# Attention and MLP on one core: x's loads spread over six head pairs, a head pair's loads moved behind the bias phase, and four small reorderings

## The chip, the cores and the metric

One core of a Trainium2 chip runs the whole program. The metric is the device time of one execution in microseconds (us); lower is better. Two times of this kernel that lie within 0.2% of each other can't be told apart.

## The reference, cut to what matters

Attention with a bias that a small network makes from relative positions, then an MLP with ELU over the attention's output (2304 tokens of 512). Sizes: batch 4, 8 heads, 576 positions, head size 64, hidden 32 for the bias, 2048 for the MLP.

```python
scores = (q @ k.transpose(0, 1, 3, 2)) / np.sqrt(D)
psi_rel = np.log1p(np.abs(pos[:, None] - pos[None, :]))
psi_i = np.log1p(np.maximum(pos[:, None], 1.0))
x = (psi_rel / psi_i)[..., None]
bias = np.maximum(x @ w1 + b1, 0.0) @ w2             # [576, 576, heads]
attn = softmax(scores + bias)                        # with the row maximum subtracted
x = (attn @ v) as [2304, 512]
h = x @ w_in
out = np.where(h > 0.0, h, np.exp(np.minimum(h, 0.0)) - 1.0) @ w_out
```

## The kernel before

The program is written in one order by hand (`manual_schedule`): each engine runs its instructions in the order of the code, and an instruction that waits holds all behind it on its engine. SP issues nearly all transfers, so SP is one queue in that sense too.

**Bias phase** (`bias_phase`). 36 sets. `relu(s)` makes four `rel` tiles of a set, one on ACT and three on DVE; `mix(s)` multiplies them on PE; `place(s)` scales the result on ACT with a column of `inv` into a `bo` tile (four buffers of two sets). Every second set a store of 576 KB moves `bo` to `bias` in SBUF; the sets 16 to 19 go to `biast` in smaller stores. Ahead of the loop stand the loads of the first head pairs' `kk` and `qq` (`load_pair`, five transfers of 576 KB in all for a pair) and of `vv` (`load_v`), the first two sets' `relu`, and four DVE copies that spread `inr` into `inv`. Behind the loop stands the load of the first block of MLP weights (`raw`, 1 MB).

**Attention** (`attention`). 16 head pairs `n`, each in five steps `i`. A step computes scores on PE (`ps`), adds the bias and takes the row minimum of the negated sum on DVE (`ss`, `nm`, line 303), takes exp on ACT, transposes on PE (`trans_p`) with copies back by ACT and DVE, and multiplies with v for the pair before (`pv`, `wv`, `xs`), whose result goes to HBM (`xd`). `sm` holds row sums; `turn` writes their reciprocals of a batch to `rd` every fourth pair. In between `decode` unpacks one weight block per pair: DVE reads `raw` (`low`, line 259; `sign`, line 263) and SP may load the next `raw` only after that.

**x for the MLP.** The first 768 tokens of x are four quarters `(r, h)`. `load_x(0, r, h)` loads a quarter of `xd` and the reciprocals `rr` of its rows (one `rr` buffer for all): three transfers for `h = 0`, nine for `h = 1`. `scale_x` multiplies them on DVE. `high_x` and `low_x` split a quarter in two parts. The table `early` says after which step these stand: the key `(-4, 1)` means the fourth pair from the end, pair 12, after step 1.

**MLP** (`mlp`). PE multiplies through `eight` (two blocks) and `seven` (the rest). `elu_next` runs two ACT operations on a product, `elu` the DVE operation of line 751, which is also the last reader of the product's bank. `aside(k)` runs planned side work after each product, among it the steps of `make_w`, which prepares the next weights (`S` sums, `wA`, `wB`). At the end of each third of the tokens six sums `acc` are copied to `os` tiles (even `t` on DVE, odd on ACT) and stored.

Of the kernel before, what the change touches and what calls it, by code (L numbers as in the profile page):

```python
# [10 lines left out]
F32 = mybir.dt.float32  # L11
# [13 lines left out]
def kernel(  # L25
# [11 lines left out]
    nc = tc.nc  # L37
    B, HP, D, _, S = qT.shape
    NT, DM = out.shape
    H = 2 * HP  # L40
    P = 128
# [37 lines left out]
    def w_bank(name):  # L79
        return wp.tile([P, 512], F32, tag="w", name=name)  # L80
# [8 lines left out]
    NP = len(pairs)  # L89
# [3 lines left out]
    def load_pair(n):  # L93
        b, hp = pairs[n]
        kk = ld.tile([P, S], F32, tag="kk", name="kk", bufs=2)
        qq = ld.tile([P, S], F32, tag="qq", name="qq", bufs=2)
        nat[n] = kk, qq

        nc.sync.dma_start(out=kk[0:D], in_=kT[b, hp, :, 0])
        yield  # L100
        nc.sync.dma_start(out=kk[D:P, 0:NCH * P], in_=kT[b, hp, :, 1, TAIL:])
        nc.sync.dma_start(out=kk[D:P, NCH * P:], in_=kT[b, hp, :, 1, 0:TAIL])
        yield
        for e in range(2):
            nc.sync.dma_start(out=qq[e * D:(e + 1) * D], in_=qT[b, hp, :, e])
            yield

    def load_v(n):
        b, hp = pairs[n]
        vv = st["v", n] = ld.tile([P, NU, D], F32, tag="vv", name="vv", bufs=3)  # L110
        nc.sync.dma_start(out=vv, in_=vt[b, hp])


    def bias_phase():
        with (
# [32 lines left out]
            for i in range(4):  # L148
                nc.scalar.dma_start(
                    out=inr[8 * i:8 * i + 8],  # L150
                    in_=cst[32 * i:32 * i + 32, NG + 2 + 4 * H:].rearrange("(s h) n -> h s n", s=4),
                )

            for n in range(2):
                for _ in load_pair(n):
                    pass
            load_v(0)
            w1c, b1c = cs[:, 0:1], cs[:, 1:2]
            W2 = cs[:, 2:]

# [13 lines left out]
            def relu(s):  # L174
                B, x = sets[s]
                rels[s] = []
                for g in range(4):
                    u = RIM - 64 * B - 16 * g - x
                    src = T[:, u:u + S]
                    b = SC[:, 4 * B + g, x:x + 1]  # L180
                    rel = bw.tile([P, S], F32, tag="rel", name="rel")
                    if g == 0:
                        nc.scalar.activation(rel, src, AF.Relu, bias=b)  # L183
                    else:
                        nc.vector.tensor_scalar(rel, src, b, 0.0, op0=ALU.add, op1=ALU.max)
                    rels[s].append(rel)
# [34 lines left out]
                        nc.sync.dma_start(out=biast[q0:q0 + 61:4], in_=src[:, o])  # L221

            AHEAD = 2
            for s in range(AHEAD):
                relu(s)
            for g in range(4):
                q = slice(32 * g, 32 * g + 32)
                nc.vector.tensor_copy(
                    inv[q].rearrange("p b s -> p s b"), inr[0:32].rearrange("p s (b g) -> p s b g", g=4)[:, :, :, g],
                )  # L230
            nc.vector.tensor_scalar(T[:, :cut], T[:, :cut], w1c, None, op0=ALU.mult)
            for s in range(NS):
                mix(s)
# [2 lines left out]
                if s + AHEAD < NS:  # L236
                    relu(s + AHEAD)
            place(NS - 1)
            decode(dp, 0, "load")

# [100 lines left out]
    def trans_p(n, u):  # L343
        pta, ptb = st["pt", n]

        ss = st["ss", n, u]
        if u < NCH:
            dst, o = (pta, u * P) if u < 2 else (ptb, (u - 2) * P)
            banks = [w_bank("wt") for r in range(2)]
            for x in range(2 * NCH):  # L350
                e, j = divmod(x, NCH)
                c = e * (S + TAIL) + j * P
                for r in range(2):
                    q = slice(r * TAIL, (r + 1) * TAIL)
                    nc.tensor.transpose(banks[r][:, x * TAIL:(x + 1) * TAIL], ss[q, c:c + P], ident[q, q])  # L355
            for r in range(2):
                d = dst[:, 0:2 * NCH, o + r * TAIL:o + (r + 1) * TAIL]
                copy = nc.vector.tensor_copy if r == 1 and u % 2 == 0 else nc.scalar.copy
                copy(d, banks[r].rearrange("p (x t) -> p x t", t=TAIL))
                yield  # L360
        else:
            o = 2 * P
            M = NCH * TAIL
            banks = [w_bank("wt") for e in range(2)]
            for j in range(NCH + 1):
                for e, w in enumerate(banks):
                    r = slice(e * TAIL, (e + 1) * TAIL)
                    if j < NCH:
                        c = j * P
                        nc.tensor.transpose(w[:, j * TAIL:(j + 1) * TAIL], ss[r, c:c + P], ident[r, r])  # L370
                    elif e == 0:
                        nc.tensor.transpose(w[r, M:M + TAIL], ss[r, NCH * P:], ident[r, r])
                    else:
                        nc.tensor.transpose(w[:, M:M + TAIL], ss[r, S - P:], ident[r, r])
            for e, w in enumerate(banks):
                r = slice(e * TAIL, (e + 1) * TAIL)
                d = pta[:, e * NCH:(e + 1) * NCH, o:o + TAIL]
                nc.scalar.copy(d, w[:, 0:M].rearrange("p (j t) -> p j t", j=NCH))
                nc.scalar.copy(pta[r, 2 * NCH, o:o + TAIL], w[r, M:M + TAIL])
                yield  # L380
# [123 lines left out]
    xo = dict(zip(("B11", "B12", "B21", "B22"), slots))  # L504
# [5 lines left out]
    def attention():  # L510
# [17 lines left out]

        V, G = nc.vector, nc.gpsimd
        early = {  # L530
            (-5, 3): [(load_x, 0, 0, 0)],
            (-4, 1): [(scale_x, 0, 0, 0, V)],
            (-4, 2): [(load_x, 0, 0, 1)],
            (-4, 4): [(scale_x, 0, 0, 1, V)],
            (-3, 0): [(load_x, 0, 1, 0)],
            (-3, 1): [(high_x, 0, "B11", xo["B11"], V.tensor_copy)],
            (-3, 2): [(scale_x, 0, 1, 0, V)],
            (-3, 3): [(load_x, 0, 1, 1), (low_x, 0, "B11", xo["B11"], V)],
            (-2, 0): [(scale_x, 0, 1, 1, V)],
            (-2, 1): [(high_x, 0, "B12", xo["B12"], V.tensor_copy)],  # L540
            (-2, 2): [(low_x, 0, "B12", xo["B12"], V)],
            (-2, 3): [(high_x, 0, "B21", xo["B21"], V.tensor_copy), (sums_x, 0, ("T1",), G)],
# [87 lines left out]
    def mlp():  # L630
        ep = ctx.enter_context(tc.tile_pool(name="ep", bufs=3))
# [17 lines left out]
        FIRST = 2  # L649
# [60 lines left out]
        def second(i, order):  # L710
            j = i // NQ
            for e, h in order:
                gh, gl = g[i, e]
                wh, wl = (
                    [ws[2 * i + e][f][:, DM:] for f in range(2)] if i < FIRST else [W2[i][:, f, e] for f in range(2)]
                )
                for t in range(3 * h, 3 * h + 3):
                    if (j, t) not in acc:
                        acc[j, t] = accp.tile([P, DM], F32, tag="acc", name="acc")
                        count[j, t] = 0  # L720
                    for x, w in ((gh, wh), (gh, wl), (gl, wh)):
                        count[j, t] += 1
                        nc.tensor.matmul(  # L723
                            acc[j, t],
                            lhsT=x[:, t * P:(t + 1) * P],
                            rhs=w,
                            start=(count[j, t] == 1),
                            stop=(count[j, t] == 6 * NQ),
                        )
                        if count[j, t] == 6 * NQ:  # L730
                            os = ep.tile([P, DM], F32, tag="os", name="os")
                            (nc.scalar.copy if t % 2 else nc.vector.tensor_copy)(os, acc[j, t])  # L732
                            t0 = 2 * j * HB + t * P
                            nc.sync.dma_start(out=out[t0:t0 + P, :], in_=os)
                        yield


# [98 lines left out]
        def at(i, k, fn, *args):  # L836
            plans.setdefault((i, k), []).append((fn, args))

        V, G = nc.vector, nc.gpsimd
# [11 lines left out]
        for i in range(FIRST, NQ + FIRST):  # L851
            q = i % NQ
            run = make_w(i)
            for e in range(2):
                at(i - 2, 0 if i - 2 < FIRST else 2, load_w, 2 * q + e, wq if i % 2 == 0 else keep)
            for k in (0, 1, 1, 2, 2, 3, 3) if i == FIRST else (0, 1, 2, 3, 4, 5, 6):
                at(i - 1, k, next, run)
            at(i, 0, next, run)
            at(i, 1, next, run)
            at(i, 3, next, run, None)  # L860
# [53 lines left out]
    with tc.manual_schedule():  # L914
        make_identity(nc, ident)
        bias_phase()
        attention()
        ph1.close()
        ps1.close()
        mlp()  # L920
# [58 lines left out]
```

## Time and profile before

| what | value |
|---|---|
| time, median of 3 runs | 708.55 us (708.1 to 709.25) |
| the profiled execution's own time | 708.4 us |
| its span, first to last instruction | 706.6 us |
| PE busy | 679.3 us, 96% of the span |
| DVE, ACT, POOL busy | 470.7, 440.6, 75.3 us |

The span is read in stages: the bias phase ends near 58 us, the head pairs run to some 319 us, and the rest is the MLP. A stage's pace is set by the engine that never waits in it, so idle time is looked for on PE first, then followed to the engine that PE waited for.

### The profile page before, as it was taken

The numbers are of one execution on the slowest core, as the hardware profiler recorded it, in microseconds if no ns is written. First come the engines' busy times: TensorE is split into PE (matmuls) and PEld (weight loads), VectorE is DVE, ScalarE is ACT, GpSimd is POOL, SyncE is SP. The second block draws the span as 40 slices with busy tenths as digits, with TensorE's granted clock in tenths as the row PEclk, the third lists the DMA queues.
The fourth block names the chain that finished last, engine by engine and source line by source line (L and its number), as shares of the span: only waits on it lengthen the run. The fifth ranks groups of instructions, "written<-read, shape, count | busy, mean of one in ns | idle before, by whom it ended". The sixth has DMA issues, their size and how long they took to land.

```text
span 706.6 us, 13181 instructions
## 1 busy us (share of the span) xinstructions
PE 679.3 (96%) x4992; PEld 508.7 (72%) x4992; DVE 470.7 (67%) x948; ACT 440.6 (62%) x953; POOL 75.3 (11%) x104
## 2 busy tenths in 40 slices
PE   5997999999999979899999999999999999999997
PEld 3434555555555545458799988999988899988896
DVE  6995767767766757875777899854456754444443
ACT  6996787787877757675665667643444644434433
POOL 0001332322233212330000000000000000000000
PEclk9999999999999999999999999999999999999999
DMA  6998655456555766625379977898684455555202
GB/s 165 222 221 210 219 176 200 159 163 205 185 187 185 222 175 195 216 103 187 81 268 333 330 260 257 317 350 310 212 306 176 164 209 212 202 207 214 88 1 89
DMA packets 49934, 144.58 MB, mean 205 GB/s; under 512 B 13376, under 2 KB 26448, under 8 KB 42192
## 3 DMA queue, kind: packets, MB, share of 16 engines
q1 hardware_dynamic: 49136, 143.44, 60.9%
q8 instruction: 39, 0.64, 0.4%
q10 hardware_dynamic: 736, 0.31, 0.2%
q14 instruction: 23, 0.19, 0.1%
HBM read 92.14 MB, written 40.97 MB: 188 GB/s over the span
## 4 chain that ended last, share of the span: by engine, by line
PE 51%; issue 1%; DVE 1%; ACT 1%; DMA 0%; SPq 0%; ACTq 0%
PE acc L723 27%; PE h L772 24%; DVE bias L497 0%; DMA out_dram<-os 0%; DVE e L751 0%; ACT e L758 0%; ACT gh L752 0%; DVE xs L486 0%; ACT bias L493 0%; DVE gl L746 0%; ACT e L757 0%; ACT xs L483 0%; DVE os L732 0%; DMA wf<-da 0%; ACT os L732 0%
## 5 line engine op out<-in xcount | busy, mean ns | idle before, releaser
L723 PE MATMUL acc<-wB,gh 128*128 128x512 f32 x528 | 171.3, 392 | 0.0
L303 DVE CUSTOM_DVE_ANT_0 ss<-ps,bias 128x576 f32<-128x576 f32 x128 | 91.8, 754 | 58.9 <-PE ps L291 50.2
L314 ACT ACTIVATE ss<-ss,nm 128x576 f32<-128x576 f32 x128 | 98.2, 769 | 36.9 <-DVE nm L303 36.4
L291 PE MATMUL ps<-kk,qq 64*128 64x288 f32 (+1 forms) x640 | 110.2, 423 | 7.9 <-DVE nm L303 7.6
L772 PE MATMUL h<-bias 128*128 128x384 f32 x552 | 111.8, 339 | 0.8 <-DVE rs L332 0.5
L723 PEld LDWEIGHTS acc<-wB,gh 128*128 128x128 f32 x528 | 98.1, 188 | 14.3
L772 PEld LDWEIGHTS h<-bias 128*128 128x128 f32 x552 | 99.6, 188 | 9.0 <-DVE e L751 1.9
L723 PE MATMUL acc<-wB,gl 128*128 128x512 f32 x264 | 103.8, 393 | 0.0
L291 PEld LDWEIGHTS ps<-kk,qq 64*128 64x128 f32 (+1 forms) x640 | 63.3, 178 | 28.2 <-DVE nm L303 12.5
L752 ACT CAST gh<-e 128x384 fp32r<-128x384 f32 x96 | 49.4, 514 | 44.8 <-DVE e L751 44.2
L757 ACT ACTIVATE e<-c 128x384 f32<-128x384 f32 x66 | 34.7, 525 | 53.4 <-DVE c L803 53.4
L746 DVE TENSOR_TENSOR gl<-e,gh 128x384 fp32r<-128x384 f32 x96 | 53.2, 554 | 18.1 <-ACT gh L752 15.8
L772 PE MATMUL h<-bias,wA 128*128 128x384 f32 x276 | 56.3, 338 | 0.9 <-issue 0.9
L751 DVE SCALAR_TENSOR_TENSOR e<-e,c 128x384 f32<-128x384 f32 x66 | 36.7, 557 | 30.1 <-ACT e L758 29.9
L757 ACT ACTIVATE e<-h 128x384 f32<-128x384 f32 x28 | 13.8, 491 | 68.3 <-PE h L772 68.3
L193 PE MATMUL bps<-rel,cs 128*32 128x288 f32 x576 | 45.5, 430 | 10.7 <-ACT rel L183 7.8
L723 PEld LDWEIGHTS acc<-wB,gl 128*128 128x128 f32 x264 | 49.5, 187 | 7.8
L399 PE MATMUL wv<-pta,vv 128*64 128x320 f32 (+1 forms) x320 | 54.4, 454 | 0.0
L772 PEld LDWEIGHTS h<-bias,wA 128*128 128x128 f32 x276 | 50.1, 188 | 5.0 <-issue 1.4
L758 ACT ACTIVATE e<-e 128x384 f32<-128x384 f32 x96 | 50.5, 526 | 3.0
L355 PEld LDWEIGHTS wt<-ident,ss 64*128 64x128 f32 x1024 | 37.5, 139 | 19.6 <-issue 13.0
L803 DVE TENSOR_TENSOR c<-h,u 128x384 f32<-128x384 f32 x66 | 36.7, 556 | 20.1 <-PE h L772 20.1
(105 smaller groups left out, 924.6 us busy)
## 6 DMA issues: line engine op xcount, KB each, us to landing
wB<-wB SPq DMA_DIRECT2D x22, 1024.0 KB, 5.0
raw<-in_wd_dram SPq DMA_DIRECT2D x16, 1024.0 KB, 11.0
bias<-wA SPq DMA_DIRECT2D x9, 1792.0 KB
wA<-wA SPq DMA_DIRECT2D x8, 1792.0 KB
wa<-wf SPq DMA_DIRECT2D x20, 512.0 KB, 4.3
bias<-bo SPq DMA_DIRECT2D x16, 576.0 KB, 6.4
wA<-bias SPq DMA_DIRECT2D x5, 1792.0 KB, 10.7
wf<-da SPq DMA_DIRECT2D x16, 512.0 KB, 3.9
```

The costliest lines, as they stand in the source:

```text
L193: nc.tensor.matmul(ps[32 * g:32 * g + 32, f, 0:HS], lhsT=W2, rhs=rel[g][:, f * HS:(f + 1) * HS], start=True, stop=True,)
L291: nc.tensor.matmul(banks[e][:, f, 0:HS] if u < NCH else banks[0][r, f, 0:HS], lhsT=qq[r, rows], rhs=kk[r, f * HS:(f + 1) * HS], start=True ...
L303: nc.vector.tensor_tensor_reduce(out=s.rearrange("p (f x) -> p f x", f=2), in0=ps[:, :, 0:HS], in1=bap.rearrange("p (f x) -> p f x", f=2), ...
L314: nc.scalar.activation(s, s, AF.Exp, bias=nm[:, e:e + 1], scale=-1.0, accum_out=sm[:, hp, col:col + 1])
L355: nc.tensor.transpose(banks[r][:, x * TAIL:(x + 1) * TAIL], ss[q, c:c + P], ident[q, q])
L399: nc.tensor.matmul(w[e * D:(e + 1) * D, 0:N], lhsT=l, rhs=r, start=(j == first), stop=(j == end))
L723: nc.tensor.matmul(acc[j, t], lhsT=x[:, t * P:(t + 1) * P], rhs=w, start=(count[j, t] == 1), stop=(count[j, t] == 6 * NQ),)
L746: nc.vector.tensor_sub(gl, t, gh.bitcast(F32))
L752: nc.scalar.copy(g[i, e][0][:, h * HB:(h + 1) * HB], t)
L757: nc.scalar.activation(t, src, AF.Relu, scale=-1.0)
L758: nc.scalar.activation(t, t, AF.Exp, scale=-1.0)
L772: nc.tensor.matmul(ps, lhsT=a[f][c], rhs=x[y][c], start=(start and k == 0), stop=(stop and k == len(todo) - 1), skip_group_check=not start,)
```

## The change

- The second head pair's `load_pair(1)` and the first `load_v(0)` move from ahead of the bias phase to behind it: the former ahead of the load of `raw`, the latter behind.
- The four `inv` copies move between `relu(0)` and `relu(1)`.
- In the last head pair, DVE takes the second copy of `trans_p` in every step, before in every second one.
- `early`: the four quarters of x are loaded and scaled over pairs 9 to 13, before 11 to 14; between a load and its scaling there is now a whole pair.
- `os` has four buffers, before three; the stores of odd `t` are issued by ACT, before by SP.
- The first `make_w` runs its steps at other products: the S sums one earlier, the split of S one later.

```diff
-            for n in range(2):
-                for _ in load_pair(n):
-                    pass
-            load_v(0)
+            for _ in load_pair(0):
+                pass
...
-            for s in range(AHEAD):
-                relu(s)
+            relu(0)
             for g in range(4):
                 q = slice(32 * g, 32 * g + 32)
                 nc.vector.tensor_copy(
                     inv[q].rearrange("p b s -> p s b"), inr[0:32].rearrange("p s (b g) -> p s b g", g=4)[:, :, :, g],
                 )
+            relu(1)
...
             place(NS - 1)
+            for _ in load_pair(1):
+                pass
             decode(dp, 0, "load")
+            load_v(0)
...
-                copy = nc.vector.tensor_copy if r == 1 and u % 2 == 0 else nc.scalar.copy
+                copy = nc.vector.tensor_copy if r == 1 and (u % 2 == 0 or n == NP - 1) else nc.scalar.copy
...
-            (-4, 2): [(load_x, 0, 0, 1)],
-            (-4, 4): [(scale_x, 0, 0, 1, V)],
+            (-6, 4): [(load_x, 0, 0, 1)],
+            (-5, 4): [(scale_x, 0, 0, 1, V), (load_x, 0, 1, 0)],
...
-                            os = ep.tile([P, DM], F32, tag="os", name="os")
+                            os = ep.tile([P, DM], F32, tag="os", name="os", bufs=4)
                             (nc.scalar.copy if t % 2 else nc.vector.tensor_copy)(os, acc[j, t])
                             t0 = 2 * j * HB + t * P
-                            nc.sync.dma_start(out=out[t0:t0 + P, :], in_=os)
+                            (nc.scalar if t % 2 else nc.sync).dma_start(out=out[t0:t0 + P, :], in_=os)
...
-            for k in (0, 1, 1, 2, 2, 3, 3) if i == FIRST else (0, 1, 2, 3, 4, 5, 6):
+            for k in (0, 0, 1, 2, 3, 3, 3) if i == FIRST else (0, 1, 2, 3, 4, 5, 6):
```

SP's queue at the start of the program, before: the second pair's `kk` and `qq` and the first `vv` stand ahead of the bias stores.

```order
L105 DMA qq<-in_q_dram 64x576 x2
L99 DMA kk<-in_k_dram 64x576
L101 DMA kk<-in_k_dram 64x512
L102 DMA kk<-in_k_dram 64x64
L105 DMA qq<-in_q_dram 64x576 x2
L111 DMA vv<-in_v_dram 128x576
L215 DMA bias<-bo 16x8x1152 x8
L221 DMA biast<-bo 16x4x576 x8
L215 DMA bias<-bo 16x8x1152 x8
L250 DMA raw<-in_wd_dram 128x2048
L111 DMA vv<-in_v_dram 128x576
L250 DMA raw<-in_wd_dram 128x2048
```

The same place in the changed program (its line numbers differ by one or two).

```order
L105 DMA qq<-in_q_dram 64x576 x2
L213 DMA bias<-bo 16x8x1152 x8
L219 DMA biast<-bo 16x4x576 x8
L213 DMA bias<-bo 16x8x1152 x8
L99 DMA kk<-in_k_dram 64x576
L101 DMA kk<-in_k_dram 64x512
L102 DMA kk<-in_k_dram 64x64
L105 DMA qq<-in_q_dram 64x576 x2
L251 DMA raw<-in_wd_dram 128x2048
L111 DMA vv<-in_v_dram 128x576 x2
L251 DMA raw<-in_wd_dram 128x2048
```

Five transfers moved from ahead of the first bias store to between the last one and `raw`, and one `vv` from ahead of it to behind `raw`.

SP's queue in head pair 12, from the load of `raw` in step 2 on, before. The nine transfers `xr` and `rr` are the quarter (0, 1), which DVE scales after step 4 of this same pair.

```order
L250 DMA raw<-in_wd_dram 128x2048
L409 DMA xd_76<-xs 128x256
L410 DMA xd_76<-xs 128x64
L448 DMA xr_3378<-xd_74 128x2x128
L452 DMA rr<-rd_78 64x2x128 x2
L448 DMA xr_3378<-xd_74 128x2x64
L452 DMA rr<-rd_78 64x2x64 x2
L448 DMA xr_3378<-xd_75 128x2x192
L452 DMA rr<-rd_79 64x2x192 x2
L111 DMA vv<-in_v_dram 128x576
L333 DMA rd_80<-rs 36x128
L412 DMA xd_76<-xs 128x256
```

The same stretch of pair 12 in the changed program. The nine transfers are now the quarter (1, 1), which DVE scales after step 4 of pair 13.

```order
L251 DMA raw<-in_wd_dram 128x2048
L410 DMA xd_76<-xs 128x256
L411 DMA xd_76<-xs 128x64
L111 DMA vv<-in_v_dram 128x576
L334 DMA rd_80<-rs 36x128
L413 DMA xd_76<-xs 128x256
L449 DMA xr_3434<-xd_74 128x2x128
L453 DMA rr<-rd_78 64x2x128 x2
L449 DMA xr_3434<-xd_74 128x2x64
L453 DMA rr<-rd_78 64x2x64 x2
L449 DMA xr_3434<-xd_75 128x2x192
L453 DMA rr<-rd_79 64x2x192 x2
```

The block went from ahead of the pair's `vv`, `rd` and `xd` transfers to behind them, and its reader went one pair later.

## Rows read from the trace of the kernel before

**Rows 1.** Page, part 2: PE's busy tenths in 40 slices of the span.

```profile
PE   5997999999999979899999999999999999999997
```

**Rows 2.** Timeline of PE; first row of pairs 11 to 15: start, us, operation.

```profile
223.83 1.43 PE L291 MATMUL ps<-kk,qq 64*128 64x288 f32 x8
...
239.03 1.43 PE L291 MATMUL ps<-kk,qq 64*128 64x288 f32 x8
...
254.84 1.81 PE L291 MATMUL ps<-kk,qq 64*128 64x288 f32 x8
...
262.78 2.96 PE L291 MATMUL ps<-kk,qq 64*128 64x288 f32 x8 [3.89 <-DVE nm L303]
...
277.55 1.77 PE L291 MATMUL ps<-kk,qq 64*128 64x288 f32 x8
...
296.00 1.36 PE L291 MATMUL ps<-kk,qq 64*128 64x288 f32 x8
```

**Rows 3.** Waits of PE, 238 to 300 us: us, times, longest.

```profile
PE ps L291 <- DVE nm L303: 5.0, 2, 3.9
PE wv L399 <- DVE xs L405: 1.1, 1, 1.1
```

**Rows 4.** Timelines of DVE and of SP's queue; in brackets idle before, releaser.

```profile
261.09 0.96 DVE L460 TENSOR_TENSOR xr<-xr,rr 128x768 f32<-128x768 f32 x1 [5.12 <-DMA rr<-rd]
...
284.51 0.96 DVE L460 TENSOR_TENSOR xr<-xr,rr 128x768 f32<-128x768 f32 x1 [4.08 <-DMA xd<-xs]
...
257.37 1.23 SPq L452 DMA_DIRECT2D rr<-rd  x2
```

**Rows 5.** Windows: PE, PEld, DVE, ACT, POOL busy, PEclk, DMA share, GB/s.

```profile
58.00:64.00 6.00, 5.01 (x54) 3.00 (x54) 4.26 (x11) 4.50 (x12) 0.49 (x2) 1.00 1.02 223
64.00:67.00 3.00, 1.43 (x22) 1.12 (x18) 0.28 (x1) 1.32 (x4) 0.00 (x0) 1.00 0.99 352
...
260.00:270.00 10.00, 7.22 (x42) 4.04 (x44) 5.40 (x12) 5.07 (x12) 1.58 (x3) 0.66 0.80 237
300.00:310.00 10.00, 10.00 (x102) 5.51 (x98) 9.23 (x18) 7.77 (x19) 3.62 (x5) 1.00 0.29 110
```

**Rows 6.** Timelines of DVE, ACT and SP's queue around the bias phase.

```profile
9.58 0.79 DVE L228 COPY inv<-inr 32x36 f32<-32x36 f32 x4
...
12.52 0.74 ACT L206 ACTIVATE bo<-bps,inv 128x576 f32<-128x576 f32 x1 [0.52 <-PE bps L193]
...
14.05 7.54 SPq L215 DMA_DIRECT2D bias<-bo  x4
...
66.72 0.76 DVE L303 CUSTOM_DVE_ANT_0 ss<-ps,bias 128x576 f32<-128x576 f32 x1 [3.54 <-issue]
...
68.75 0.69 DVE L259 TENSOR_SCALAR dm<-raw 128x1024 int32<-128x1024 uint32 x1 [0.59 <-DMA raw<-in_wd_dram]
```

**Rows 7.** Timelines of ACT and PE at the end of head pair 15.

```profile
315.71 1.07 ACT L359 COPY ptb<-wt 128x512 f32<-128x512 f32 x2 [0.27 <-PE wt L355]
...
316.84 1.95 PE L399 MATMUL wv<-ptb,vv 128*64 128x256 f32 x16 [0.58 <-ACT ptb L359]
```

**Rows 8.** Timelines of DVE and PE in the first MLP blocks.

```profile
336.92 0.42 DVE L682 TENSOR_TENSOR S<-wa 128x256 f32<-128x256 f32 x1
...
337.06 2.37 PE L772 MATMUL h<-bias 128*128 128x384 f32 x12 [0.21 <-DVE e L751]
...
346.21 0.55 DVE L751 SCALAR_TENSOR_TENSOR e<-e,h 128x384 f32<-128x384 f32 x1
...
346.86 1.29 PE L772 MATMUL h<-bias,wA 128*128 128x384 f32 x6 [0.95 <-issue]
```

**Rows 9.** Timeline of ACT at the end, and one row of the last chain.

```profile
699.32 0.59 ACT L732 COPY os<-acc 128x512 f32<-128x512 f32 x1 [4.03 <-PE acc L723]
...
702.94 0.59 ACT L732 COPY os<-acc 128x512 f32<-128x512 f32 x1 [0.78 <-DMA out_dram<-os]
...
700.72 2.07 DMA out_dram<-os
```

More of the change, by code (lines that the diff above doesn't have):

```diff
@@ L530, in attention @@
         early = {
-            (-5, 3): [(load_x, 0, 0, 0)],
-            (-4, 1): [(scale_x, 0, 0, 0, V)],
-            (-4, 2): [(load_x, 0, 0, 1)],
-            (-4, 4): [(scale_x, 0, 0, 1, V)],
-            (-3, 0): [(load_x, 0, 1, 0)],
+            (-7, 3): [(load_x, 0, 0, 0)],
+            (-6, 3): [(scale_x, 0, 0, 0, V)],
+            (-6, 4): [(load_x, 0, 0, 1)],
+            (-5, 4): [(scale_x, 0, 0, 1, V), (load_x, 0, 1, 0)],
+            (-4, 4): [(scale_x, 0, 1, 0, V), (load_x, 0, 1, 1)],
             (-3, 1): [(high_x, 0, "B11", xo["B11"], V.tensor_copy)],
-            (-3, 2): [(scale_x, 0, 1, 0, V)],
-            (-3, 3): [(load_x, 0, 1, 1), (low_x, 0, "B11", xo["B11"], V)],
-            (-2, 0): [(scale_x, 0, 1, 1, V)],
+            (-3, 2): [(low_x, 0, "B11", xo["B11"], V)],
+            (-3, 4): [(scale_x, 0, 1, 1, V)],
             (-2, 1): [(high_x, 0, "B12", xo["B12"], V.tensor_copy)],
```

## The prediction

> **What bounds the kernel now.** I read the slices of the page first, then PE's timeline, then PE's waits, then the engines that PE waited for. PE is at nine tenths or more in nearly every slice of 17.7 us [rows 1], in the MLP in all but the last, so there is next to nothing to be had there. What can be had lies in the dips: the first slice, the fourth (53 to 71 us, the end of the bias phase and pair 0), two late in the attention (247 to 265 us and 283 to 300 us), and the last.
>
> PE's timeline gives the pace of the head pairs. Pair 11 runs from 223.83 to 239.03, which is 15.20 us, without idle time [rows 2]. Pairs 12, 13 and 14 start at 239.03, 254.84 and 277.55, and pair 15 at 296.00: 15.81, 22.71 and 18.45 us, 56.97 together, where three paced pairs would take 45.60. So these three pairs, which hold x's loads and scalings, cost **11.37 us** over the pace. PE's waits there are 5.0 us for DVE's `nm` (one of 3.9, one of 1.1) and 1.1 us for DVE's `xs` [rows 3]. DVE in turn stood 5.12 us and 4.08 us before a `scale_x`, waiting for transfers [rows 4]: the nine issues of an `h = 1` quarter take SP 0.62 us each (two in 1.23), 5.5 us in all, and the scaling stood two steps behind them. The waits are not the whole price: in the 10 us around the long one the granted clock was 0.66, between the two levels of 1.2 and 2.4 GHz, after PE had stood idle 3.89 us [rows 2, 5], and the row after that idle time takes 2.96 us, against 1.43 to 1.81 of the rows that head pairs.
>
> **x's loads.** The change removes no operation. It puts a whole pair, 15.2 us, between each quarter's load and its scaling; nine issues need 5.5 us and the landing some 2 us more (an `out` store lands in 2.07 [rows 9], the nearest row), so both DVE waits should go, with the idle PE and the low clock behind them. What stays is the DVE time of x itself. Pair 14 bounds it: 18.45 less 15.20 less its two waits of 1.1 is 1.05 us for five x operations there (one scaling, two `high_x`, two `low_x`), 0.21 each. After the change ten such operations lie in pairs 10 to 14: at most 2.1 us, and at least nothing, if they fall into idle DVE time. I take 1.7, since pairs 10 and 11 were at the pace and now get a scaling each. Gain: 11.37 - 1.7 = **9.7 us** (9.3 to 11.4). Behind a `load_x` whose `rr` waits for the scaling just ahead of it, SP queues the next pair's `kk` and `qq`; these are needed a pair later and have the room.
>
> **The second pair's loads behind the bias.** Two effects. The first bias store is issued at 14.05, although its second `place` ended at 12.52 + 0.74 = 13.26 [rows 6]: SP was still issuing the loads. From there the DMA engines are full up to 67 us (share 1.02 and 0.99 [rows 5]), and DVE's wait at 66.72 (3.54 us) names no engine, so what is left is the landing of the last store: the stream is late. So the stream moves 14.05 - 13.26 = 0.8 us earlier. But 576 KB (0.59 MB) now stand between the last bias store and `raw`: at the 352 GB/s of 64 to 67 us that is 1.7 us. DVE takes `raw` at 68.75 after waiting 0.59 us for it, and the fourth step's `ss`, hence pair 1, stands behind that instruction. The stall on the bias gets 0.8 shorter, the one on `raw` longer, and `raw` decides: **+0.9 us**. Bounds: -0.8, if the loads fit into gaps of the stream; +2.6, if they move at the 223 GB/s of 58 to 64 us and the stream starts no earlier. I take the rate of the row in which reads from HBM run. `load_v(0)` is wanted only by pair 1's `pv`, after `raw`, and costs nothing unless it lands over 2 us behind it.
>
> The row shows `raw` served after the bias stores that were issued ahead of it. The Trainium skill ("DMA: Bandwidth & Descriptors", section "Queues, rings and completion order") says that on each DMA engine the descriptors of one queue are consumed in ring order. By it all five loads are paid for ahead of `raw`, the +0.9; if SP's queue were not served in order, the sum would be up to 1.7 us lower. The rule speaks against this part of the change.
>
> **The `inv` copies.** Four copies of 0.79 us in all change places with three `rel` operations [rows 6]; DVE's total stays. The second `place`, which waited for PE, hides it; without that cover 0.8 us. I take 0.
>
> **The copies of the last pair.** At the end PE waits 0.58 us for ACT's two copies, 1.07 us one after the other [rows 7]; side by side they end about 0.4 earlier. In the step before, DVE is at 9.23 of 10 us [rows 5] and gets another copy (0.5 us as on ACT), ahead of an `ss` that PE waits for. I set them against each other: 0 (-0.5 to +0.5).
>
> **The first `make_w`.** PE waits 0.95 us at 346.86 for the bank that DVE frees at 346.21 + 0.55 [rows 8]; DVE was held there by the split of S, which waits for ACT and now comes a product later. That wait goes. In exchange the two S sums (0.42 us each) move ahead of the operation for which PE already waits 0.21 at 337.06, so about 0.75 of it shows there. Net **-0.2** (-0.95 to +0.8).
>
> **The end.** The last `os` copy starts at 702.94, after 0.78 us of waiting for a store to free a buffer [rows 9]. With four buffers it needs the second store's: the copy of 699.32 ends at 699.91, its store lands 2.07 later, 701.98. So up to 0.96 earlier; the last sum itself is ready near 702, and I take **-0.85** (0, if stores that ACT issues land that much later, to -0.96). The ACT issues of the earlier thirds delay ELU by about the 0.6 us of an SP issue, where ACT is idle half the time; PE never waited there: 0.
>
> **Sum.** -9.7 + 0.9 - 0.2 - 0.85 = -9.85 on the profiled execution's 708.4 us (span 706.6 and 1.8 around it): 698.55. The median of the runs shown is 0.15 above it, so I predict **698.7 us**.
>
> **Rivals.**
> - The scalings cost in full. Four scalings of 0.96 us [rows 4] land in pairs that had no DVE stall, and if each pushes `ss` and so PE by its whole length, that is 3.8 beside the 2.1 for what is left: gain 5.5, time 702.9. For it: DVE runs in order and PE follows `nm`. Against: pair 15 carries x work too at DVE 9.23 of 10, with PE full [rows 5].
> - The second pair's loads are free. The store stream leaves gaps, `raw` comes 0.8 earlier with it: 697.0. For it: the five loads are issued while the last stores are still in flight. Against: the DMA share is 0.99 to 1.02 throughout.
> - **Slower than before:** SP becomes the bound. A block of nine issues (5.5 us) stands ahead of the next pair's `kk` and `qq` and holds until the scaling ahead of it is done; if these reach SBUF after their pair's start, PE stops. It decides when the block is held for more than the 15.2 us less 5.5 and some 5 us of the five loads, thus by over 4.7 us; three blocks that miss by 5.5 each cost 16.5 and a time near 715. Against: a block of nine already stood ahead of those loads in pair 12, and the pair they are for, 14, starts without idle PE [rows 2].
> - The change does not do what it says: if the waits of 5.12 and 4.08 were for `xd` or `rd` written late, and not for the issues, an earlier place does not help and the time is 708.3. Against: the first quarters read batches 0 and 1, finished pairs earlier.
>
> **How the numbers follow.** My forecast 0.70, scalings in full 0.12, loads free 0.13, SP as the bound 0.03, no effect 0.02. The predicted time is the first one's. The bounds of the terms give 694 to 703; the first three cases lie between 697.0 and 702.9, and with about 1 in 10 left out on either side the range is 696.0 to 702.2. Measurement tells 0.2%, 1.4 us, from no change: faster 0.95, the same 0.02, slower 0.03.
>
> **What would show it.** Right: in the changed profile pairs 12, 13 and 14 take 15.2 to 16 us each, no `scale_x` waits over 0.5 us, the clock stays at 1.00 from 250 to 280 us; DVE takes `raw` near 69.6; PE waits about 0.9 us near the spot of 337.06 and none at that of 346.86 (both some 9 us earlier); the last copy follows the last sum. Wrong: pairs 10 and 11 over 16 us (scalings in full), `raw` before 68.5 (loads free), idle PE at a pair's start on a transfer (SP).

## The result, and the profile after

The changed kernel takes **700.9 us** (median of 4 runs, 700.37 to 701.67) against 708.52 of the kernel before on the same chip: ratio 0.989 (0.9875 to 0.9909), 7.6 us faster. The profiled execution took 701.14 us, with a span of 699.4, 7.2 shorter than before. That is 2.2 above the 698.7 predicted, and inside the predicted range.

The x loads first. The first score products of head pairs 2 and 10 to 15 on PE's timeline after (they answer to [rows 2]; line numbers are one or two higher than before):

```profile
90.38 1.43 PE L292 MATMUL ps<-kk,qq 64*128 64x288 f32 x8
...
212.74 1.43 PE L292 MATMUL ps<-kk,qq 64*128 64x288 f32 x8
227.95 1.77 PE L292 MATMUL ps<-kk,qq 64*128 64x288 f32 x8
243.49 1.43 PE L292 MATMUL ps<-kk,qq 64*128 64x288 f32 x8
258.69 1.79 PE L292 MATMUL ps<-kk,qq 64*128 64x288 f32 x8
274.52 1.35 PE L292 MATMUL ps<-kk,qq 64*128 64x288 f32 x8
289.92 1.37 PE L292 MATMUL ps<-kk,qq 64*128 64x288 f32 x8
```

Pairs 12, 13 and 14 take 15.20, 15.83 and 15.40 us, 46.43 where it was 56.97. Pairs 10 and 11 take 15.21 and 15.54, 0.35 over the pace. So this part brought 10.54 - 0.35 = **10.2 us**. DVE's scalings stand with no idle time ahead of them (they answer to [rows 4]), and the clock is whole (PEclk is the third number from the right; [rows 5] had 0.66):

```profile
244.33 0.95 DVE L461 TENSOR_TENSOR xr<-xr,rr 128x768 f32<-128x768 f32 x1
259.72 0.95 DVE L461 TENSOR_TENSOR xr<-xr,rr 128x768 f32<-128x768 f32 x1
275.36 0.95 DVE L461 TENSOR_TENSOR xr<-xr,rr 128x768 f32<-128x768 f32 x1
...
240.00:270.00 30.00, 30.00 (x315) 17.45 (x311) 24.73 (x55) 22.90 (x61) 9.07 (x12) 1.00 0.71 220
270.00:310.00 40.00, 39.68 (x404) 22.44 (x400) 33.84 (x69) 31.47 (x80) 15.40 (x17) 1.00 0.58 190
```

Pair 2, though, starts at 90.38; before it was 86.29. The start lost **4.1 us**, where the prediction had 0.9. DVE's timeline there (answers to [rows 6]):

```profile
65.91 0.76 DVE L304 CUSTOM_DVE_ANT_0 ss<-ps,bias 128x576 f32<-128x576 f32 x1 [3.34 <-DMA kk<-in_k_dram]
66.60 0.08 DVE L304 DVE_READ_ACCUMULATOR2_ANT nm<- 128x1 f32 x1
66.60 0.75 DVE L304 CUSTOM_DVE_ANT_0 ss<-ps,bias 128x576 f32<-128x576 f32 x1
67.28 0.08 DVE L304 DVE_READ_ACCUMULATOR2_ANT nm<- 128x1 f32 x1
70.34 0.69 DVE L260 TENSOR_SCALAR dm<-raw 128x1024 int32<-128x1024 uint32 x1 [2.98 <-DMA raw<-in_wd_dram]
70.95 0.75 DVE L304 CUSTOM_DVE_ANT_0 ss<-ps,bias 128x576 f32<-128x576 f32 x1
```

The bias came at 65.91 instead of 66.72, but `raw` at 70.34 instead of 68.75, and two `ss` stand behind it on DVE. PE waits for them, and comes back slow:

```profile
66.74 1.67 PE L292 MATMUL ps<-kk,qq 64*128 64x288 f32 x7 [1.91 <-DVE nm L304]
...
71.76 2.96 PE L292 MATMUL ps<-kk,qq 64*128 64x288 f32 x8 [1.89 <-DVE nm L304]
74.66 1.87 PE L400 MATMUL wv<-pta,vv 128*64 128x320 f32 x6
...
66.00:68.00 2.00, 1.26 (x6) 0.78 (x8) 1.36 (x4) 1.28 (x3) 0.00 (x0) 1.00 1.05 290
68.00:70.00 2.00, 1.76 (x20) 1.11 (x16) 0.00 (x0) 1.18 (x6) 0.24 (x1) 0.65 0.97 384
70.00:74.00 4.00, 2.24 (x7) 1.81 (x8) 3.66 (x7) 2.21 (x5) 2.17 (x2) 0.50 0.12 44
74.00:78.00 4.00, 4.00 (x21) 1.45 (x20) 2.08 (x6) 1.91 (x5) 2.81 (x3) 0.50 0.82 285
```

The eight score products take 2.96 us at a granted clock of 0.50, the 1.2 GHz level, where [rows 2] show 1.36 to 1.81 at full clock (the prediction's lower end of 1.43 leaves out pair 15). Before, the clock read 1.00 in all of 56 to 92 us. From pair 1's first product to pair 2's, before first, then after (PE's busy time is the second number):

```profile
70.17:86.29 16.12, 16.12 (x162) 9.39 (x159) 12.84 (x27) 12.14 (x32) 5.43 (x7) 1.00 0.65 208
```

```profile
71.76:90.38 18.62, 18.62 (x159) 10.78 (x159) 12.62 (x27) 12.46 (x32) 5.18 (x7) 0.81 0.58 184
```

PE has no idle time in either. So the 4.1 us are two: pair 1 starts 1.6 us later (71.76 instead of 70.17), and takes 2.5 us longer at a granted clock of 0.81.

Where the moved loads went shows in two windows of each kernel, before first, then after (the last two numbers are DMA share and GB/s):

```profile
0.00:14.00 14.00, 6.18 (x60) 4.22 (x64) 8.29 (x23) 7.58 (x12) 0.70 (x6) 1.00 0.54 136
14.00:56.00 42.00, 39.17 (x521) 16.32 (x513) 40.63 (x95) 41.18 (x64) 0.00 (x0) 1.00 1.02 227
```

```profile
0.00:14.00 14.00, 6.34 (x63) 3.47 (x65) 8.45 (x23) 8.18 (x13) 0.70 (x6) 1.00 0.47 113
14.00:56.00 42.00, 42.00 (x517) 20.33 (x514) 40.48 (x95) 41.10 (x64) 0.00 (x0) 1.00 1.01 220
```

They left a stretch in which the DMA engines were half busy, and the start of the full one, for the end of the full one: by these rates 0.3 MB less moved up to 14 us ((136 - 113) GB/s over 14 us) and 0.3 MB less from 14 to 56 ((227 - 220) GB/s over 42 us), of the 0.88 MB that the five loads and the `vv` hold. In 64 to 67 us, where they now run, the rate is 225 GB/s, where [rows 5] have 352:

```profile
64.00:67.00 3.00, 1.09 (x17) 0.89 (x14) 1.09 (x3) 1.00 (x3) 0.00 (x0) 1.00 1.05 225
```

The rest in one profile each: from pair 15's first product to the MLP's 23.72 us, before 23.47. In the first MLP blocks (answers to [rows 8]):

```profile
313.64 0.58 PE L772 MATMUL h<-bias 128*128 128x384 f32 x2 [0.47 <-DVE rs L333]
...
331.88 2.37 PE L772 MATMUL h<-bias 128*128 128x384 f32 x12 [0.84 <-DVE e L751]
...
340.36 1.23 PE L772 MATMUL h<-bias,wA 128*128 128x384 f32 x6
```

The wait of 0.21 us became 0.84, the one of 0.95 went. From 313.64 to 340.36 are 26.72 us, before 27.39 (from 319.47 to 346.86): 0.7 less. From the first `os` copy to the end of the span are 7.28 us (692.12 to 699.4), before 7.96 (698.64 to 706.6): 0.7 less. So 4.1 - 10.2 + 0.25 - 0.7 - 0.7 = -7.25, the 7.2 of the spans.

### The profile page after: what moved, and what is told of

The parts are those of the page before. It is cut to its first block, busy times and chain, and to the rows that moved or that the text cites. A ratio compares the mean times of both kernels' runs of the same rounds, so it can differ in the third digit from the quotient of the medians.

```text
span 699.4 us, 13181 instructions
## 1 busy us (share of the span) xinstructions
PE 680.6 (97%) x4992; PEld 512.2 (73%) x4992; DVE 472.0 (67%) x950; ACT 439.7 (63%) x951; POOL 76.3 (11%) x104
## 4 chain that ended last, share of the span: by engine, by line
PE 92%; DMA 2%; DVE 2%; issue 1%; ACT 1%; SPq 1%; ACTq 0%; DVEq 0%
PE acc L723 28%; PE h L772 24%; PE wv L400 13%; PE ps L292 12%; PE bps L191 7%; PE wt L356 5%; PE wm L341 2%; DMA raw<-in_wd_dram 1%; PE wt L371 1%; DMA T<-in_rtab_dram 1%; DVE ss L304 0%; DVE bias L498 0%; DMA out_dram<-os 0%; SPq L101 0%; DVE e L751 0%
## 5 line engine op out<-in xcount | busy, mean ns | idle before, releaser
L191 PE MATMUL bps<-rel,cs 128*32 128x288 f32 x576 | 48.0, 424 | 7.7 <-ACT rel L181 7.7
L803 DVE TENSOR_TENSOR c<-h,u 128x384 f32<-128x384 f32 x66 | 36.7, 557 | 20.1 <-PE h L772 20.1
```

The source lines that it names most:

```text
L191: nc.tensor.matmul(ps[32 * g:32 * g + 32, f, 0:HS], lhsT=W2, rhs=rel[g][:, f * HS:(f + 1) * HS], start=True, stop=True,)
```

## The experiments

Theory: the start lost its 4 us through the second pair's loads alone, which put `raw` and pair 1's data behind a full DMA stretch, leave PE idle, and bring the low clock. Rivals: another part lost it, or x gained less than its rows say. Every ratio is to the kernel before on the same chip.

**1. Undo that part, from the changed kernel.**

```diff
-            for _ in load_pair(0):
-                pass
+            for n in range(2):
+                for _ in load_pair(n):
+                    pass
+            load_v(0)
...
-            for _ in load_pair(1):
-                pass
             decode(dp, 0, "load")
-            load_v(0)
```

> The changed kernel with load_pair(1) and load_v(0) back ahead of the bias phase; all else as changed. Theory (the five loads ahead of raw make raw land 1.6 us later than before, and the longer idle time of PE lowers its clock, 2.5 us more): DVE takes raw near 68.7 again instead of 70.34, the granted clock stays at 1.00 from 66 to 80 us, pair 2 starts near 86.3 instead of 90.38, and the time falls by about 4 us, to 697. Rival (the low clock comes from the inv copies between the relus, or by chance): pair 2 still starts over 88 and the time falls by at most 1.6 us, to 699.3 or more.

**696.49 us**, ratio 0.982 (0.9801 to 0.9835). DVE and PE:

```profile
65.54 0.76 DVE L303 CUSTOM_DVE_ANT_0 ss<-ps,bias 128x576 f32<-128x576 f32 x1 [2.37 <-PE wt L374]
...
67.56 0.69 DVE L259 TENSOR_SCALAR dm<-raw 128x1024 int32<-128x1024 uint32 x1 [0.58 <-DMA raw<-in_wd_dram]
...
66.36 1.67 PE L291 MATMUL ps<-kk,qq 64*128 64x288 f32 x7 [0.93 <-DVE nm L303]
...
68.98 1.91 PE L291 MATMUL ps<-kk,qq 64*128 64x288 f32 x8
```

Pair 1 starts 2.8 us earlier than after, at full clock, pair 2 at 85.10, 5.3 us earlier. It beats both kernels.

**2. `raw` ahead of the second pair's loads**, all still behind the bias.

```diff
+            decode(dp, 0, "load")
             for _ in load_pair(1):
                 pass
-            decode(dp, 0, "load")
```

> The changed kernel with the load of raw issued ahead of load_pair(1), both still behind the bias phase. Theory (what hurts is the 0.59 MB ahead of raw on the one queue): raw is taken at 67.3 to 68.5, pair 1 starts by 69.5 to 70.5, clock 1.00, time 696 to 697.5. Rival (what hurts is that pair 1's own kk and qq come late, wherever raw stands): they now land after raw, PE stands at pair 1's start for them beyond 70.5 us, and the time stays within 1 us of 700.9.

699.75 us, 0.986 (0.9845 to 0.9877). `raw` is taken at 69.52, and now the other part of the queue is late: pair 1's first product waits for its own `qq`.

```profile
71.48 1.79 PE L292 MATMUL ps<-kk,qq 64*128 64x288 f32 x8 [1.50 <-DMA qq<-in_q_dram]
```

So neither of the two orders tried behind the bias is good; with experiment 1 it is the place that costs.

**3. That part alone, on the kernel before** (the two hunks of experiment 1, reversed).

> The kernel before with nothing changed but load_pair(1) and load_v(0) moved behind the bias phase. Theory: that part alone costs the 4.1 us by which pair 2 started later (90.38 against 86.29): 712.6. By the step of the prediction (0.9 us, raw late and no more): 709.4. Rival (the inv copies bring the loss): 708.5.

712.5 us, 1.004 (1.0028 to 1.0055): slower, by 2.9 us (2.0 to 3.9), less than the 4.1 expected. In its profile `raw` is taken at 71.01 after 2.99 us, and pair 2 starts at 91.21, 4.9 us later than before.

**4. The table of x alone, on the kernel before** (the diff's hunk on `early`).

> The kernel before with nothing changed but the places of x's loads and scalings in the table early. Theory (pairs 10 to 14 lose their waits: 10.2 us by the traces): 698.3, no scale_x waiting over 0.5 us, clock 1.00 from 250 to 280 us. By the step of the prediction (9.7): 698.8. Rival (the shift of the whole attention by the late start took part in it, since DVE and SP met otherwise): a gain of under 8 us, 700.5 or more.

698.42 us, 0.984 (0.9828 to 0.9857): 11.1 us faster (10.1 to 12.2). Pairs 12 to 14 take 15.20, 15.85 and 15.39 us:

```profile
239.71 1.43 PE L291 MATMUL ps<-kk,qq 64*128 64x288 f32 x8
...
254.91 1.80 PE L291 MATMUL ps<-kk,qq 64*128 64x288 f32 x8
...
270.76 1.35 PE L291 MATMUL ps<-kk,qq 64*128 64x288 f32 x8
```

**5. The score sets ahead of `raw` on DVE**: the first operation on `raw` goes one step later; the loads stay where the change put them.

```diff
-            if i == (1 if n > 0 else 3):
+            if i == (1 if n > 0 else 4):
                 d(this, "scale", "low")
```

> The changed kernel (700.9), with VectorE's first operation on the decode's load raw in head pair 0 moved behind the last two score sets of that pair, so that these no longer stand behind a wait for raw; SP's order of loads is unchanged. If the 4.1 us that head pair 2 starts late come from two score sets queued on VectorE behind the wait of 2.98 us (head-of-line), the sets run from 68.4, head pair 1's first product moves from 71.76 to about 69.5, head pair 2 from 90.4 to 87 to 88, and the time is 697.5 to 698.8. If head pair 1's own kk and qq are as late as raw, its first product stays above 71 with a wait on a DMA, and the time is 700 to 701. The granted clock was 0.65 in 68:70 of the changed kernel, before the wait for raw ended: if it still falls here, about 1 us more is lost than in the first case (698.8 to 699.8).

699.88 us, 0.988 (0.9859 to 0.9897): by time not told apart from the changed kernel. In the trace `ss` goes ahead of `raw`, as meant, and pair 1's products start before `raw` is there:

```profile
67.37 0.76 DVE L304 CUSTOM_DVE_ANT_0 ss<-ps,bias 128x576 f32<-128x576 f32 x1 [4.51 <-DMA qq<-in_q_dram]
...
69.78 0.76 DVE L304 CUSTOM_DVE_ANT_0 ss<-ps,bias 128x576 f32<-128x576 f32 x1 [0.97 <-PE ps L292]
...
71.71 0.69 DVE L260 TENSOR_SCALAR dm<-raw 128x1024 int32<-128x1024 uint32 x1 [0.48 <-DMA raw<-in_wd_dram]
...
71.02 1.59 PE L292 MATMUL ps<-kk,qq 64*128 64x288 f32 x4
```

But the bias came 1.5 us later than in the changed kernel's profile, with the same loads. One profile's start scatters that much, so the table below counts from the bias.

**6. Work for idle PE.** Results of the extra products are not used.

```diff
+        if (n, u) in ((0, 3), (1, 0)):
+            k0, q0 = nat[0]
+            fill = v_bank("wv")
+            for f in range(3):
+                nc.tensor.matmul(
+                    fill[:, 0:HS], lhsT=q0[:, 0:P], rhs=k0[:, (f % 2) * HS:(f % 2 + 1) * HS],
+                    start=True, stop=True,
+                )
```

> The changed kernel with two groups of three extra products (288 columns, results in an idle accumulator bank that nothing reads before it is written again) ahead of the two products of TensorE that wait 1.91 and 1.89 us at 66.74 and 71.76. The waits themselves stay. If the low granted clock (0.50 in 70:78) follows from TensorE's idling there and costs 2 to 2.5 us of the 4.1, the clock reads 1.00 in 68:82, head pair 2 starts near 88 and the time is 698.4 to 699. If the clock hides behind other waits, the clock is 1.00 and the time stays at 700.5 to 701.2. If idle TensorE is not what lowers the clock, it stays at 0.50 and the time stays too.

698.82 us, 0.987 (0.9854 to 0.9891): by time not told apart from the changed kernel either. The low clock did not vanish but ended earlier. The last line is pair 1, from its first product to pair 2's, at full clock:

```profile
70.00:72.00 2.00, 2.00 (x18) 1.57 (x18) 0.45 (x1) 0.59 (x4) 0.48 (x2) 0.50 0.80 305
72.00:74.00 2.00, 2.00 (x8) 1.23 (x8) 2.00 (x6) 1.04 (x3) 1.22 (x1) 0.70 0.04 16
74.00:78.00 4.00, 4.00 (x41) 2.49 (x42) 3.29 (x7) 2.46 (x6) 3.13 (x2) 1.00 0.50 172
...
73.83:89.09 15.26, 15.26 (x160) 9.01 (x159) 11.91 (x25) 11.29 (x30) 4.94 (x6) 1.00 0.69 228
```

**7. Experiments 5 and 6 together.**

> Both edits together: the first decode operation behind head pair 0's last score sets, and extra products (results unused) ahead of the two waiting ones. Counted from the end of VectorE's wait for the bias to head pair 2's first product, so that the bias's own scatter drops out: 19.6 us in the kernel before, 24.5 in the changed one, 21.8 with either edit alone. If the queueing behind raw and the low clock are two costs, together they leave 19.6 to 20.5 here, the clock is 1.00, and the time is 697 to 698.5. If they are one and the same cost (a shorter wait is also a shorter idle stretch), it stays at 21.5 to 22 and the time at 698.5 to 700. If head pair 1's own loads are what remains, its first product shows a wait on a DMA for kk or qq.

699.37 us, 0.989 (0.9869 to 0.9918). The clock is 1.00 throughout, yet pair 2 starts 21.9 us after the bias. The extra products spoiled the experiment: with `raw` out of the way they no longer fill idle time but stand in the path, from 71.34 to 72.99, while DVE had freed the two banks at 71.04 and 71.72. Less these 1.3 to 1.65 us it would be 20.3 to 20.6; that is worked out, not shown.

**8. The end: four buffers, all stores on SP.**

```diff
-                            (nc.scalar if t % 2 else nc.sync).dma_start(out=out[t0:t0 + P, :], in_=os)
+                            nc.sync.dma_start(out=out[t0:t0 + P, :], in_=os)
```

> The changed kernel with its four output buffers, but all six last stores on SP. If the buffers gave the tail its 0.7 us, the last store is issued as before this edit, 4.1 us after the first output copy's start (692.12 to 696.26), and the span stays within 0.2 us of 699.4. If the second queue gave it, the distance is about 4.9 again and the span 0.7 longer.

700.83 us in one run, span 699.1. The last `os` copy starts 3.53 us after the first, as in the changed kernel, and the span ends 7.27 us after the first (changed: 7.28).

**9. The end: three buffers, two queues** (`bufs=4` taken out).

> The changed kernel with three output buffers, odd stores still on ScalarE's queue. If the buffers gave the tail its 0.7 us, the fourth output copy waits for the first store to land (0.7 us), and the last store is issued about 4.8 us after the first output copy's start; the span is 0.6 to 0.8 longer. If the queue gave it, 4.1 us as in the changed kernel.

701.88 us in one run, span 700.1. ACT in the changed kernel, then here:

```profile
694.16 0.59 ACT L732 COPY os<-acc 128x512 f32<-128x512 f32 x1 [0.77 <-PE acc L723]
...
695.65 0.58 ACT L732 COPY os<-acc 128x512 f32<-128x512 f32 x1 [0.90 <-DMA out_dram<-os]
```

```profile
695.07 0.58 ACT L732 COPY os<-acc 128x512 f32<-128x512 f32 x1 [1.67 <-DMA out_dram<-os]
...
696.45 0.58 ACT L732 COPY os<-acc 128x512 f32<-128x512 f32 x1 [0.80 <-DVE os L732]
```

The first copy started at 692.12 and 692.14, so the last comes 0.8 later with three buffers, and the span ends 7.96 us after the first, as before the change. The fourth buffer makes the whole gain, the second queue none.

**10. The last pair's copies back on ACT**, from experiment 1's kernel (`or n == NP - 1` taken out).

> The version with the second head pair's loads ahead of the bias phase (696.5), and the last pair's transposed copies back on ScalarE where they were. From head pair 15's first product to the MLP's first: 23.46 us in the three profiles with the old copies so far, 23.72 in the six with the new ones. If the copies are the cause, 23.46 here and 0.25 us less in time, which the rounds cannot resolve. If another part is, 23.72.

696.18 us, 0.985 (0.9823 to 0.9873). From pair 15's first product to the MLP's are 23.46 us, as in the four others with the old copies (before, 3, 4 and 12: 23.46 or 23.47); nine with the new ones (changed, 1, 2, 5 to 9, 11) show 23.71 to 23.73. The copies cost 0.25.

**11. The inverse's copies back behind both relus**, from experiment 1's kernel.

```diff
-            relu(0)
+            for s in range(AHEAD):
+                relu(s)
...
-            relu(1)
```

> The version with the second head pair's loads ahead of the bias phase (696.5), and the inverse's four copies back behind both relus. The prediction's zero says: the first bias store is issued within 0.8 us of 13.57 and the time stays within 0.7 of 696.5. If the earlier copies let the bias phase start earlier, the first copy starts near 9.5 instead of 8.2, the wait for the bias ends about 1 us later (66.5 instead of 65.5), and the time is 697.2 to 697.8.

697.79 us, 0.987 (0.9836 to 0.9897): 1.3 above experiment 1 and, on the same chip, 1.6 above experiment 10, with intervals that overlap, and the bias at 66.36 where experiments 1 and 10 had 65.54 and 65.03. That looked like an effect that the prediction had put at nothing, so the part was run alone.

**12. The inverse's copies alone, on the kernel before** (experiment 11's hunk, reversed).

> The kernel before with the inverse's four copies between the first two relus, and nothing else changed. The prediction's zero says: ScalarE places the last set at the same time (its last store's placement started at 56.1 to 56.3 in the profiles with the loads ahead, with the old copies and with the new), the wait for the bias ends near 66.5 as in the three profiles with the old copies (66.72, 66.54, 66.36), and the time is within 0.7 us of the kernel before. If the earlier copies really bring the bias in earlier, the wait ends at 65.0 to 65.6 as in the two profiles with the new copies (65.54, 65.03), and the time is 1.0 to 1.5 us below before.

708.79 us, 1.000 (0.998 to 1.0024): no effect in time. The bias did come early, at 65.59, but so it scatters; pair 2 then started later, at 87.49, since here the low clock came too (0.70, 0.50 and 0.59 in 68:70, 70:74 and 74:76). Its pair 1, with the loads ahead of the bias phase as before:

```profile
69.15:87.49 18.34, 18.34 (x161) 10.49 (x159) 12.61 (x27) 12.45 (x32) 5.42 (x7) 0.82 0.59 184
```

All starts in one table, from one profile each: the end of DVE's wait for the bias, when DVE takes `raw`, pair 2's first product, the time from the bias to pair 1's first product, the time from there to pair 2's, the sum of the two (the distance), and the clock's loss (what the granted clock is short of 1.00, times the window's length, over windows of 2 us from 56 to 92). Of experiment 3's loss, 1.7 lie ahead of the bias. That DVE's wait ends with the bias is read from experiment 2, whose profile names that store (`bias<-bo`, 3.58 us); the others name another row or none, and in 3 and 10 a PE row ended within 0.02 us of it, so there the bias may have come earlier.

| kernel | bias | raw | pair 2 | bias to pair 1 | pair 1 | distance | clock's loss, us |
|---|---|---|---|---|---|---|---|
| before | 66.72 | 68.75 | 86.29 | 3.5 | 16.1 | 19.6 | 0 |
| 1, loads ahead | 65.54 | 67.56 | 85.10 | 3.4 | 16.1 | 19.6 | 0 |
| 10, loads ahead | 65.03 | 67.09 | 84.65 | 3.5 | 16.1 | 19.6 | 0 |
| 11, loads ahead | 66.36 | 68.94 | 86.67 | 4.0 | 16.3 | 20.3 | 0 |
| 4, loads ahead | 66.54 | 68.43 | 86.60 | 4.0 | 16.0 | 20.1 | 1.7 |
| 12, loads ahead | 65.59 | 67.72 | 87.49 | 3.6 | 18.3 | 21.9 | 3.4 |
| changed | 65.91 | 70.34 | 90.38 | 5.9 | 18.6 | 24.5 | 5.1 |
| 3 | 66.57 | 71.01 | 91.21 | 5.9 | 18.8 | 24.6 | 5.1 |
| 8 | 67.51 | 71.85 | 90.88 | 5.8 | 17.6 | 23.4 | 5.1 |
| 9 | 66.76 | 71.17 | 89.86 | 5.8 | 17.3 | 23.1 | 3.4 |
| 2, raw first | 66.44 | 69.52 | 88.59 | 5.0 | 17.1 | 22.2 | 1.7 |
| 5, ss ahead of raw | 67.37 | 71.71 | 89.18 | 3.7 | 18.2 | 21.8 | 1.7 |
| 6, extra products | 67.33 | 71.55 | 89.09 | 6.5 | 15.3 | 21.8 | 1.7 |
| 7, both | 67.86 | 72.12 | 89.78 | 5.1 | 16.8 | 21.9 | 0 |

With the loads ahead the distance is 19.6 to 20.3, save for experiment 12 with its low clock; with them behind and nothing else done (changed, 3, 8, 9) it is 23.1 to 24.6, and `raw` comes 4.3 to 4.4 us after the bias instead of 1.9 to 2.6. The bias itself ends at 65.0 to 66.7 with the loads ahead and at 65.9 to 67.9 with them behind, 1.0 later in the mean (six and eight profiles), where the prediction had it 0.8 earlier.

## Why the prediction was right, and where its sizes were off

The main term is right in its mechanism and its size. That the time is only 2.2 us off is in part luck: the start alone is 3.2 us worse than predicted, beyond its own bound, while x and `make_w` came out 0.5 better each.

- **x's loads**: predicted -9.7, measured -10.2 on the profile, and alone (experiment 4) 10.2 on its profile and 11.1 (10.1 to 12.2) by time. The mechanism holds as told: no `scale_x` waits, no idle PE in pairs 10 to 14, clock 1.00. The rival "scalings cost in full" falls: all that x's operations can have cost is the 0.35 us of pairs 10 and 11 and the 0.83 that 13 and 14 take over the pace, 1.2 us together where 1.7 was predicted.
- **The second pair's loads**: the mis-sized term, and the reason that the time is 2.2 above the forecast. Predicted +0.9 with an upper bound of +2.6, measured +4.1, and 5.3 by the undoing. The step that failed is "`raw` decides: +0.9 us". The way is right (`ss` and pair 1 stand behind `raw`), but it gave the price of the queue too low and left the clock out. (1) Pair 1 starts 1.6 us later. In this profile the bias did come 0.8 earlier, but `raw` follows it by 4.4 us instead of 2.0: 2.4 us for 0.59 MB, thus 246 GB/s, where the prediction took 352 from a row in which the loads were not there. Nor can the earlier bias be put down to the earlier stream: the first store is issued at 12.50 instead of 14.05, but over all profiles the bias ends 1.0 us later. I looked at what stood behind the loads' new place and not at how cheap the old one was. (2) Pair 1 takes 2.5 us longer, at the low clock; the prediction had nothing for this. I had read the low clock after idle time in [rows 2, 5] and used it for x, where it goes, but not here, where it comes.
- What the part costs by time is less sharp: alone 2.9 us (2.0 to 3.9, experiment 3), by the undoing about 5.2 (ratios 0.989 and 0.982, on two chips). The low clock may make part of this difference, which is argued and not shown: over whole executions the granted clock was 0.985 to 0.988 in experiment 3's six runs, but 0.985 to 0.995 in those of the kernel before on the same chip.
- **The clock.** The table splits the loss into a queue and a clock. From the bias to pair 1's first product it takes 3.4 to 4.0 us with the loads ahead, and 5.8 to 5.9 with them behind and nothing else done. Pair 1 itself takes 16.1 to 16.3 us at full clock (before, 1, 10, 11), and 17.3 to 18.8 at a granted clock of 0.81 to 0.88 (changed, 3, 8, 9). That this second part is the clock's and not the queue's, two profiles show: experiment 12, with the loads ahead and no longer queue, has 18.34 us at 0.82; experiment 6, with `raw` 4.2 us behind the bias, has 15.26 at 1.00 (even less than the 16.1 of the others; why is not shown). Experiment 5 is the reverse: the queue is gone (3.65 us from the bias to pair 1), the clock is not (pair 1 at 0.93, with another idle time of 0.67 us in it). Nor does the low clock come by chance of one profile: over whole executions it was 0.992 or 0.993 in all four runs of the changed kernel, and 0.998 or 0.999 in all four of experiment 1. Why it fell in experiment 12 and in no profile of 1, 10 and 11 stays open.
- SP's queue is served in order: put ahead of the five loads, `raw` is taken 3.1 us after the bias instead of 4.4, and `qq` is late in its place (experiment 2). The rival "loads free" is out. The Trainium skill ("DMA: Bandwidth & Descriptors", section "Queues, rings and completion order") has the descriptors of one queue consumed in ring order on each DMA engine; these runs agree. The order is not all, though: even ahead of the loads `raw` comes 3.1 us after the bias, where it is 1.9 to 2.6 without them.
- **The inverse's copies**: predicted 0, measured 0 (experiment 12).
- **The last pair's copies**: predicted 0 (-0.5 to +0.5), measured +0.25 in every profile. PE's wait of 0.58 us for ACT went, as foreseen, but PE now waits 0.3 us for `nm` and 0.3 for `sm`, two waits on DVE that the old copies don't have.
- **`make_w`**: predicted -0.2, measured -0.7 in this profile. The two waits came as foreseen (0.84, and none). From the MLP's first product to the one at 342.58 it is 29.6 us in the mean of four profiles with the old order (before, 3, 4, 12; 29.0 to 29.9), 29.0 in ten with the new (28.2 to 29.5): about -0.6. No run had this part alone.
- **The end**: predicted -0.85, measured -0.7. The last copy still waits 0.90 us for a store, where I had expected it ready with the last sum; the reason, the buffer, is shown by 8 and 9.

SP never became the bound. The best version is the change without its first part: 696.2 to 696.5 us (experiments 10 and 1), and the two can't be told apart.

## What to carry to other kernels

Before a load is moved out of the way of a stream, read the DMA share on both sides: here 0.59 MB that left a half-idle stretch for the end of a full one cost 2.4 us there and held up everything queued behind. Price a wait on PE with the clock that may follow it, also where you add the wait, not only where you remove it. And where a stage's end is set by transfers at full share, as the bias's is here, one profile can scatter by a microsecond or more (65.03 to 66.72 with the loads ahead): count from the event that ends the stage, and run a part alone before you believe an effect of that size.

## What the runs showed of the hardware that was not expected

Full clock did not follow the length of PE's idle time by a simple rule. The kernel before stood idle 2.10 us ahead of the product at 67.54 and kept 1.00; experiment 4, idle 2.06 us ahead of 67.36, fell to 0.53 in 68:70 and 0.62 in 70:72; experiment 12, idle 1.53 us ahead of 66.41, fell as well. In the changed kernel, with two such times (1.91 and 1.89), it fell to 0.65 in 68:70, ahead of the second, read 0.50 for some 8 us, and came back while PE was busy without a gap. What pair 1 paid is plain in the rows: 16.12 us at 1.00, 18.34 to 18.78 at 0.81 or 0.82, without idle time in either. The bias stream, full in either kernel, moved 227 GB/s in 14:56 before and 220 after, and ended anywhere between 65.03 and 67.86.
